# Reading two activations back by blocks, and loading the first expert's gates earlier in the DMA queue

## The chip, the core and the metric

The kernel runs on one core of one Trainium2 chip. The metric is the device time of one execution in microseconds (us), as the median of several runs. The core's engines run side by side and wait for each other by semaphores: PE (TensorE, matrix products; PEld is its loading of weights), DVE (VectorE), ACT (ScalarE), POOL (GpSimd) and SP (SyncE), whose queue issues every DMA of this kernel. A DMA on that queue is issued when all before it have been issued and its own waits are over.

## The reference

Four batches (b = 0 to 3) of 576 tokens go through attention on a memory, a dense layer and four experts:

```python
attn_out = _attn_ref(**attn_kwargs)             # 4 batches x 8 heads x 576 x 64
x = attn_out.transpose(0, 2, 1, 3).reshape(B * S, H * D)   # 2304 x 512
h = x @ w_in                                    # dense: 512 -> 2048
g = np.maximum(h, 0.0) + alpha * np.minimum(h, 0.0)
x = g @ w_out                                   # 2048 -> 512
p = domain_probs / (domain_probs.sum(-1, keepdims=True) + 1e-09)
for e in range(E):                              # four experts, 512 -> 1024 -> 512
    h = np.maximum(x @ w1[e], 0.0)
    out += p[:, e:e + 1] * (h @ w2[e])
```

## The kernel before

**Two stages.** The first stage (attention and the dense layer) is recorded task by task from a string, `ORDER`: each name is a task, and the order of the names is the order of the instructions on every engine. Each float32 operand is split into a high and a low part of a type that PE takes at full rate, and a product is made in three passes (high by high, high by low, low by high); hence the helpers `hi` (ACT) and `lo` (DVE or POOL). The second stage (`run_experts`) is a plain loop. It runs over 32 units: for half 0 (batches 0 and 1) and half 1 (batches 2 and 3), over eight groups of 512 expert columns, over the two batches of the half. Unit 0 is group 0 with batch 0; unit 15 is the last of half 0 (group 7, batch 1), unit 16 the first of half 1 (group 0, batch 2).

**A unit.** It has two passes, hp = 0 and 1. In each, class `Up` makes the first expert product by a seven-product (Strassen-like) scheme on 2 by 2 blocks: `p1` to `p7` write PE's accumulators `ux`, `uy`, `uw`; `v1`, `v16`, `v167` copy or add them into small tiles `v`; `c11`, `c12`, `c21`, `c22` write the four blocks of `h`. `gate` (DVE) multiplies `h` by the tile `p` with the tokens' gates, and `hi` and `lo` split the result into `g`. Between them class `Down` makes the second product of the unit before, eight products `o`, each added to `acc` by `flush`. A product of `Up` is six matmuls (one set) and one of `Down` twelve (two sets), so a unit has 14 + 16 = 30 sets; unit 0, with no unit before it, has 14. Weights go through POOL and ACT in half 0 and are stored to memory (`keep`, tiles `kw`); half 1 reads them back (`w1_load`, `w2_load`).

**Places.** The functions in `more` are recorded at the places (hp, 0) to (hp, 4) of a unit: (hp, 0) follows `v16`, (hp, 1) follows `p2` and `c11`, (hp, 2) follows `v167` and `c22`, (hp, 3) follows the gate of blocks 2 and 3, (hp, 4) follows `p3` and `c12`.

**Activations.** The dense layer's results `y` of batches 2 and 3 don't fit beside the experts' tiles: `spill` stores them (DRAM tiles `ysp2`, `ysp3`), and `unspill` reads each back into one tile `yu` of 128 by 2304 floats (9216 bytes a partition) in a pool `yt` with one buffer. From it class `Combos` makes the seven operands of the scheme: four differences (`sum`, DVE, tiles `xt`) and their splits (`hi` on ACT, `lo` on DVE or POOL, tiles `x`). It does so during unit 15 for batch 2 and unit 16 for batch 3. The tile for batch 3 takes the buffer of batch 2's, so its read waits for the last reader of that.

**Gates.** `store_gates` writes all gates to a DRAM tile `pd` in the first stage. `load_gates(e, b)` reads those of expert e and batch b into a tile `p` of 128 by 576. The first two calls stand at the head of `run_experts`, so their DMAs stand on SP behind all that `ORDER` recorded: behind the load of raw weights `raww21`, the store of the split weights `kw101` (1792 KB, line L713), and `ysp3` (1152 KB).

**Memory.** `to_experts` closes the first stage's pools and opens the experts' pools in the same bytes (`hp`, `vp` and `pp` hold `h`, `v` and `p`). A new tile waits for the last users of the old tiles whose bytes it takes.

Of the kernel before, what the change touches and what calls it, by code (L numbers as in the profile page):

```python
# [8 lines left out]
F32 = mybir.dt.float32  # L9
# [12 lines left out]
HB = S // 2  # L22
# [148 lines left out]
n125 v124 h124 v125 x1h5 d123  # L171
l124 h125 x1l5 x1h6 l125 u126 e123 u127 n126 n127 v126 d124
x1l6 h126 x1h1 v127 d125
l126 h127 x1l1 x1h2 l127 to wh01 d126
x1l2 d127
wl01 e127 sp3
"""
# [14 lines left out]
def memory_attention_experts(ctx: ExitStack, tc: tile.TileContext, phi, q, kv, w_in, w_out, w1, w2, alpha, dp, out):  # L192
# [7 lines left out]
    nc = tc.nc  # L200
# [21 lines left out]
    def unit(name, dt=F32, pool=big):  # L222
        return pool.tile([128, UNIT], dt, tag="big", name=name)
# [289 lines left out]
    wp_t, pw_t, y_t, x_t = {}, {}, {}, {}  # L513
# [106 lines left out]
    B11, T2, T1, B21, T3, T4, B22 = range(7)  # L620
    y_spill = {b: dram.tile([128, UNIT], F32, name=f"ysp{b}") for b in (2, 3)}
# [2 lines left out]
    def spill(b):  # L624
        nc.sync.dma_start(out=y_spill[b], in_=y_t[b].rearrange("p d n -> p (d n)"))

    def unspill(b):
        y_t[b] = unit(f"yu{b}", pool=pools["y"]).rearrange("p (d n) -> p d n", d=4)
        nc.sync.dma_start(out=y_t[b].rearrange("p d n -> p (d n)"), in_=y_spill[b])

    def operand(b, i):

# [5 lines left out]
    class Combos:  # L638
# [3 lines left out]
            self.b, self.t = b, {}  # L642

        def block(self, i, j):
            return y_t[self.b][:, 2 * i:2 * i + 2, j * HB:(j + 1) * HB]

        def sum(self, n):
# [26 lines left out]
    pools = {}  # L674
# [4 lines left out]

    def to_experts():  # L680
        early.close()
        for name, key, bufs in (("w1b", ("w1", 1), 1), ("hp", "h", 2), ("vp", "v", 1), ("pp", "p", 2), ("ring2", "w2", 6), ("accp", "acc", 2), ("yt", "y", 1), ("xt", "xt", 2)):
            pools[key] = ctx.enter_context(tc.tile_pool(name=name, bufs=bufs, reuse_waits="tile"))

    sums_t, kept_t = {}, {}
# [48 lines left out]
    def load_gates(e, b):  # L734
        t = p_t[e, b] = pools["p"].tile([128, S], F32, tag="p", name=f"p{e}{b}")
        src = pd.rearrange("e p i -> e (p i)")[e:e + 1, b * S:(b + 1) * S]
        nc.sync.dma_start(out=t, in_=src.to_broadcast([128, S]))
# [122 lines left out]
                nc.sync.dma_start(out=out[rows, b * S:(b + 1) * S], in_=acc_t[b][:, d])  # L860

    def run_experts():
        load_gates(0, 0)
        load_gates(0, 1)
        units = [(half, g, 2 * half + t) for half in range(2) for g in range(NG) for t in range(2)]
        last, old = None, None
        for n_unit, (half, g, b) in enumerate(units):
            t = b % 2

            more = {}  # L870
            after = units[n_unit + 1:n_unit + 3]
            if t == 0 and n_unit and not half:
                more[0, 1] = [(w1_hi, g, 1)]
                more[0, 2] = [(w1_lo, g, 1)]
            if t == 1 and len(after) > 1:
                nh, ng = units[n_unit + 1][:2]
                if nh:
                    for hp in range(2):
                        more[hp, 1] = [(w1_load, g, ng, hp, 0, 2), (w1_load, g, ng, hp, 3, 5)]
                        more[hp, 3] = [(w1_load, g, ng, hp, 5, 6), (w1_load, g, ng, hp, 2, 3)]  # L880
                        more[hp, 4] = [(w1_load, g, ng, hp, 6, 7)]
                else:
                    more[0, 3] = [(w1_sums, ng, 0)]
                    more[1, 0] = [(w1_hi, ng, 0)]
                    more[1, 1] = [(w1_lo, ng, 0)]
                    more[1, 4] = [(w1_sums, ng, 1)]
            w2 = [(w2_load if half else w2_split, g, hp) for hp in range(2)]
            if t == 0:
                more.setdefault((1, 1), []).extend(f + (0,) for f in w2)
            else:  # L890
                more.setdefault((0, 0), []).extend(f + (1,) for f in w2)
            if n_unit > 1:

                h0, g0, b0 = units[n_unit - 1]
                h1, g1, b1 = units[n_unit + 1] if n_unit + 1 < len(units) else (None, None, None)
                if g0 % 2 == 1 and h1 is not None:
                    more.setdefault((0, 0), []).append((load_gates, g1 // 2, b1))
            if (half, g) == (0, 1) and t == 0:
                more.setdefault((0, 4), []).append((unspill, 2))
            for bb, u0 in ((2, (0, NG - 1, 1)), (3, (1, 0, 0))):  # L900
                if (half, g, t) == u0:
                    x = Combos(bb)
                    parts = [
                        ((0, 0), [(x.sum, 0), (x.sum, 1), (x.hi, B11)]),
                        ((0, 1), [(x.lo, B11, nc.gpsimd), (x.hi, T2), (x.hi, T1)]),
                        ((0, 2), [(x.lo, T1, nc.vector), (x.sum, 2), (x.lo, T2, nc.gpsimd)]),
                        ((0, 3), [(x.sum, 3), (x.hi, B21), (x.hi, T4)]),
                        ((0, 4), [(x.lo, B21, nc.gpsimd), (x.lo, T4, nc.vector)]),
                        ((1, 0), [(x.hi, T3)]),
                        ((1, 1), [(x.lo, T3, nc.vector)]),  # L910
                        ((1, 2), [(x.hi, B22)]),
                        ((1, 3), [(x.lo, B22, nc.vector)] + ([(unspill, 3)] if bb == 2 else [])),
                    ]
                    for place, fs in parts:
                        more.setdefault(place, []).extend(fs)

            for hp in range(2):
                u = Up(g, b, hp)
                side = iter(range(0, 3) if hp == 0 else range(3, 8))

                def down():
                    if old:
                        n = next(side)
                        old.product(n)
                        old.flush(n)

                def extra(place):
                    for f, *args in more.get((hp, place), ()):
                        f(*args)

                u.p1()
                u.p6()
                u.v1()
                if last:

                    if hp == 0:
                        last.hi(1)
                    last.gate(0)
                    last.hi(0)
                u.v16()  # L940
                if last:
                    if hp == 0:
                        last.lo(1, nc.vector)
                    last.lo(0, nc.vector if hp == 0 else nc.gpsimd)
                extra(0)
                if hp == 1:
                    down()
                u.p5()
                u.p2()
                u.c11()  # L950
                if hp == 1:
                    down()
                extra(1)
                u.p7()
                u.v167()
                u.c22()
                extra(2)
                down()
                u.p4()
                u.c21()  # L960
                u.gate(1)
                if hp == 0:
                    u.hi(1)
                    u.lo(1, nc.gpsimd)
                extra(3)
                down()
                u.p3()
                u.c12()
                extra(4)
                down()  # L970
                last = u
            old = Down(g, b)
        last.gate(0)
        for i in (1, 0):
            last.hi(i)
            last.lo(i, nc.vector)
        for n in range(8):
            old.product(n)
            old.flush(n)
# [18 lines left out]
    def task(name, fn, *args):  # L998
        tasks[name] = fn, args
# [66 lines left out]
    for kind in ("in", "out"):  # L1066
        for i in range(DFF // 128):
            d = Decode(kind, i)
            parts = [d.sign, d.first, d.second, d.third, d.add] + ([] if kind == "in" else [d.split, d.split2])
# [6 lines left out]
    task("pst", store_gates)  # L1076
    task("wopen", open_w1)
    task("to", to_experts)

    with tc.manual_schedule():  # L1080
        make_identity(nc, ident)
        nc.gpsimd.memset(mask, 0.0)
        for h in range(4):
            nc.gpsimd.memset(mask[32 * h:32 * h + 32, h % 2:h % 2 + 1], 1.0)
        for name in ORDER.split():
            run(name)
        run_experts()
# [45 lines left out]
```

## Time and profile before

| | before |
|---|---|
| median of 3 runs | 1193.4 us (1193.06 to 1196.33) |
| profiled execution: its own time, its span | 1195.45 us, 1193.6 us |
| mean granted TensorE clock, share of full speed | 0.989 |
| PE busy | 1165.7 us, 98% of the span |
| DVE, ACT, POOL busy | 62%, 35%, 25% |
| DMA | 157.98 MB moved, 37.2% of 16 engines' span |

The span reaches from the first to the last instruction; the time around it is 1.85 us. Busy shares are means over the whole span; what a stage waits for is in the rows below. Lines are those of the kernel before (L841 is a line of `Down.product`).

### The profile page before, as it was taken

Reading aid. Unit: us, or ns where it says so; the run is one execution under the profiler, and the core shown is the slowest. Engines: PE = TensorE matmul, PEld = TensorE weight load, DVE = VectorE, ACT = ScalarE, POOL = GpSimd, SP = SyncE. Lnnn points to the kernel's source line nnn. Section 1 sums busy time; section 2 is a strip of 40 time slices with the busy share of each in tenths; the row PEclk is TensorE's granted clock in tenths of the full one; section 3 lists DMA queues with packets and bytes.
Section 4 is the critical chain, followed back from the end, with each engine's and each line's share of the span. In section 5 each row is a group of like instructions: output and inputs, shape, how many; then the busy total and the mean of one; then the engine's idle time right before and its main releaser. Section 6 shows DMA issues by size and latency. Waiting matters only on the chain.

```text
span 1193.6 us, 21493 instructions
## 1 busy us (share of the span) xinstructions
PE 1165.7 (98%) x8796; PEld 1122.0 (94%) x8796; DVE 744.9 (62%) x1403; ACT 422.9 (35%) x953; POOL 302.3 (25%) x263
## 2 busy tenths in 40 slices
PE   8899999999999899999999999989999999999998
PEld 7578999999999899999999999989999999999998
DVE  6999888885567544656556566665455455545553
ACT  5567665554455334232223232322221111111110
POOL 2332023221010062553434525421001100110010
PEclk9999999999999989999999999989999999999999
DMA  9641121301000446445454444544353433433411
GB/s 378 256 172 27 64 90 53 107 22 77 1 1 4 175 128 230 175 164 197 166 174 172 168 170 163 191 163 165 131 152 123 133 126 93 156 113 138 160 46 70
DMA packets 51667, 157.98 MB, mean 132 GB/s; under 512 B 5360, under 2 KB 18672, under 8 KB 47600
## 3 DMA queue, kind: packets, MB, share of 16 engines
q1 hardware_dynamic: 51568, 156.60, 37.2%
q8 instruction: 69, 1.13, 0.4%
q14 instruction: 30, 0.25, 0.1%
HBM read 103.33 MB, written 53.25 MB: 131 GB/s over the span
## 4 chain that ended last, share of the span: by engine, by line
PE 92%; DVE 4%; DMA 2%; issue 1%; ACT 1%; SPq 0%; POOL 0%; DVEq 0%; ACTq 0%; POOLq 0%
PE o L841 34%; PE y L600 16%; PE uy L750 13%; PE ux L750 8%; PE uw L750 8%; PE h L562 8%; PE pw L523 2%; DMA rawin<-in_w_in 1%; DMA p<-pd 1%; DMA yu<-ysp 1%; DVE xt L660 1%; PE y L597 1%; PE pm L325 0%; PE pc L357 0%; DVE rs L395 0%
## 5 line engine op out<-in xcount | busy, mean ns | idle before, releaser
L853 DVE TENSOR_TENSOR acc<-o,acc 128x288 f32<-128x288 f32 x224 | 102.4, 457 | 202.8 <-PE o L841 202.8
L841 PE MATMUL o<-g,w 128*128 128x288 f32 x1536 | 226.8, 297 | 0.0
L841 PE MATMUL o<-g,w2l 128*128 128x288 f32 x1536 | 223.6, 295 | 1.1 <-DVE g L232 1.1
L841 PEld LDWEIGHTS o<-g,w 128*128 128x128 f32 x1536 | 212.8, 190 | 0.0
L841 PEld LDWEIGHTS o<-g,w2l 128*128 128x128 f32 x1536 | 210.0, 188 | 1.6 <-DVE g L232 1.6
L600 PE MATMUL y<-g,wout 128*128 128x288 f32 x1440 | 205.5, 297 | 0.0
L600 PEld LDWEIGHTS y<-g,wout 128*128 128x128 f32 x1440 | 194.2, 188 | 10.5 <-issue 7.0
L750 PE MATMUL uy<-x,w 128*128 128x288 f32 x1152 | 186.3, 297 | 8.2 <-DVE v L784 8.2
L232 POOL TENSOR_TENSOR g<-h,g 128x576 fp32r<-128x576 f32 x64 | 92.3, 1444 | 388.5 <-ACT g L819 388.5
L750 PEld LDWEIGHTS uy<-x,w 128*128 128x128 f32 x1152 | 165.3, 190 | 9.3 <-DVE v L784 9.3
L788 ACT COPY v<-ux 128x288 f32<-128x288 f32 x64 | 25.6, 401 | 308.3 <-PE ux L750 308.3
L819 ACT CAST g<-h 128x576 fp32r<-128x576 f32 x128 | 83.3, 676 | 138.6 <-DVE h L813 138.6
L750 PE MATMUL ux<-x,w 128*128 128x288 f32 x768 | 124.0, 297 | 4.8 <-ACT v L788 4.8
L750 PE MATMUL uw<-x,w 128*128 128x288 f32 x768 | 123.3, 296 | 0.0
L750 PEld LDWEIGHTS ux<-x,w 128*128 128x128 f32 x768 | 109.9, 190 | 5.0 <-ACT v L788 5.0
L813 DVE SCALAR_TENSOR_TENSOR h<-h,p 128x576 f32<-128x576 f32 x128 | 104.7, 818 | 8.8 <-DMA p<-pd 5.6
L750 PEld LDWEIGHTS uw<-x,w 128*128 128x128 f32 x768 | 109.6, 189 | 0.0
L232 POOL TENSOR_TENSOR w<-raww,w 128x512 fp32r<-128x512 f32 (+1 forms) x48 | 74.5, 1566 | 137.8 <-ACT w L507 77.6
L562 PE MATMUL h<-a,wp 128*128 128x288 f32 x720 | 108.8, 296 | 0.1
L784 DVE TENSOR_TENSOR v<-uy,v 128x288 f32<-128x288 f32 x128 | 58.6, 457 | 80.5 <-PE uy L750 80.2
L562 PEld LDWEIGHTS h<-a,wp 128*128 128x128 f32 x720 | 99.5, 188 | 2.7 <-issue 1.3
L581 DVE SCALAR_TENSOR_TENSOR pos<-neg,nal,pos 128x288 f32<-128x288 f32 x120 | 64.8, 544 | 43.0 <-ACT pos L576 42.4
(117 smaller groups left out, 1125.4 us busy)
## 6 DMA issues: line engine op xcount, KB each, us to landing
kw<-w SPq DMA_DIRECT2D x16, 1792.0 KB, 7.2
raww<-in_w SPq DMA_DIRECT2D x32, 512.0 KB, 4.0
kw<-w SPq DMA_DIRECT2D x32, 512.0 KB, 2.9
w<-kw SPq DMA_DIRECT2D x32, 512.0 KB, 4.8
w2l<-kw SPq DMA_DIRECT2D x32, 512.0 KB, 4.5
w<-kw SPq DMA_DIRECT2D x48, 256.0 KB, 3.8
kv<-in_kv SPq DMA_DIRECT2D x8, 1152.0 KB, 12.0
rawin<-in_w_in SPq DMA_DIRECT2D x16, 512.0 KB, 3.7
```

The costliest lines, as they stand in the source:

```text
L232: eng.tensor_tensor(out=out, in0=in0, in1=in1.bitcast(F32), op=ALU.subtract)
L523: mm(p[64 * j:64 * j + 64, g * 256:(g + 1) * 256], vt_t[b, g][:, j, :], win_t[c][:, 2 * g + j, e * 256:(e + 1) * 256], start=True, stop=True,)
L562: mm(p, wp_t[b, c, f // 2][:, x, o2 + g * 256:o2 + g * 256 + 128], a_t[b][:, y, g, o:o + HB], start=(n == 0), stop=(n == 5))
L581: nc.vector.scalar_tensor_tensor(out=pos, in0=neg, scalar=nal[:, ft:ft + 1], in1=pos, op0=ALU.mult, op1=ALU.add)
L600: mm(First.acc[d], w[:, x, d * 128:(d + 1) * 128], self.gt[:, y, 0:HB], start=(self.start and n == 0), stop=(self.stop and n == 2))
L750: mm(p, w[:, x, a, k], operand(self.b, i)[:, y, k], start=(start and n == 0), stop=(n == 5), skip_group_check=not start)
L784: nc.vector.tensor_tensor(out=out, in0=x, in1=y, op=ALU.add)
L788: nc.scalar.copy(out=self.v1_t, in_=self.x)
L813: nc.vector.scalar_tensor_tensor(out=h, in0=h, scalar=0.0, in1=p_t[self.g // 2, self.b], op0=ALU.max, op1=ALU.mult)
L819: nc.scalar.copy(out=g_t[self.g, self.b, self.hp][:, i, 0], in_=h)
L841: mm(self.p, w[:, x, i, d % 2 * 128:(d % 2 + 1) * 128], g, start=(m == 0), stop=(m == 11))
L853: nc.vector.tensor_tensor(out=a, in0=self.p, in1=a, op=ALU.add)
```

## The change

`pp` is opened ahead of `hp` and `vp`, so the tiles `p` take other bytes of the closed pools. The two loads of the first expert's gates become tasks `pg0` and `pg1` in `ORDER`, right behind `to`, and leave the head of `run_experts`. `yt` gets four buffers of a quarter each, and `unspill` reads one quarter (a block of 128 by 2 by 288, 288 KB, in runs of 1152 bytes). Batch 2's four blocks are read at one place as before (unit 2). Batch 3's are read at four places of unit 15, (0, 2), (0, 4), (1, 1) and (1, 4), in place of one read at (1, 3).

```diff
-l126 h127 x1l1 x1h2 l127 to wh01 d126
+l126 h127 x1l1 x1h2 l127 to pg0 pg1 wh01 d126
...
-    def unspill(b):
-        y_t[b] = unit(f"yu{b}", pool=pools["y"]).rearrange("p (d n) -> p d n", d=4)
-        nc.sync.dma_start(out=y_t[b].rearrange("p d n -> p (d n)"), in_=y_spill[b])
+    def unspill(b, i, j):
+        t = y_t[b, i, j] = pools["y"].tile([128, 2, HB], F32, tag="y", name=f"yu{b}{i}{j}")
+        src = y_spill[b].rearrange("p (d n) -> p d n", d=4)
+        nc.sync.dma_start(out=t, in_=src[:, 2 * i:2 * i + 2, j * HB:(j + 1) * HB])
...
         def block(self, i, j):
+            if self.b > 1:
+                return y_t[self.b, i, j]
             return y_t[self.b][:, 2 * i:2 * i + 2, j * HB:(j + 1) * HB]
...
-        for name, key, bufs in (("w1b", ("w1", 1), 1), ("hp", "h", 2), ("vp", "v", 1), ("pp", "p", 2), ("ring2", "w2", 6), ("accp", "acc", 2), ("yt", "y", 1), ("xt", "xt", 2)):
+        for name, key, bufs in (("w1b", ("w1", 1), 1), ("pp", "p", 2), ("hp", "h", 2), ("vp", "v", 1), ("ring2", "w2", 6), ("accp", "acc", 2), ("yt", "y", 4), ("xt", "xt", 2)):
...
     def run_experts():
-        load_gates(0, 0)
-        load_gates(0, 1)
...
-                more.setdefault((0, 4), []).append((unspill, 2))
+                more.setdefault((0, 4), []).extend((unspill, 2, i, j) for i in range(2) for j in range(2))
...
-                        ((1, 3), [(x.lo, B22, nc.vector)] + ([(unspill, 3)] if bb == 2 else [])),
+                        ((1, 3), [(x.lo, B22, nc.vector)]),
                     ]
+                    if bb == 2:
+                        parts += [(place, [(unspill, 3, i, j)]) for place, i, j in (((0, 2), 0, 0), ((0, 4), 0, 1), ((1, 1), 1, 0), ((1, 4), 1, 1))]
...
+    for b in range(2):
+        task(f"pg{b}", load_gates, 0, b)
```

The orders of PE, DVE, ACT and POOL stay as they were. Only SP's order changes. At the border of the stages it was as follows (`p00` and `p01` are the gates of expert 0 for batches 0 and 1, `kw2000` is the first store of unit 0's split weights):

```order
L713 DMA kw100_3455<-w100_3433 128x3584
L625 DMA ysp2_108<-y2_1498 128x2304
L438 DMA raww21_5110<-in_w2 128x1024
L713 DMA kw101_5112<-w101_5080 128x3584
L625 DMA ysp3_109<-y3_1787 128x2304
L737 DMA p00_5119<-pd_107 128x576
L737 DMA p01_5121<-pd_107 128x576
L713 DMA kw2000_5222<-w2000_5219 128x1024
```

After the change the two gate loads stand ahead of `raww21`, `kw101` and `ysp3`, right behind `ysp2`:

```order
L717 DMA kw100_3455<-w100_3433 128x3584
L625 DMA ysp2_108<-y2_1498 128x2304
L741 DMA p00_5080<-pd_107 128x576
L741 DMA p01_5082<-pd_107 128x576
L438 DMA raww21_5114<-in_w2 128x1024
L717 DMA kw101_5116<-w101_5084 128x3584
L625 DMA ysp3_109<-y3_1787 128x2304
L717 DMA kw2000_5222<-w2000_5219 128x1024
```

In unit 15, SP reads group 0's weights back (`w170`, `w171`) and stores parts of the output (`out_0`). Before, the one read of batch 3's activation stood near the end of these:

```order
L720 DMA w170_8585<-kw100_3455 128x2x256 x2
L860 DMA out_0<-acc0_5328 128x576
L720 DMA w170_8585<-kw100_3455 128x2x256
L860 DMA out_0<-acc0_5328 128x576
L720 DMA w171_8747<-kw101_5112 128x2x512 x2
L860 DMA out_0<-acc0_5328 128x576
L720 DMA w171_8747<-kw101_5112 128x2x256 x2
L629 DMA yu3_9218<-ysp3_109 128x2304
L720 DMA w171_8747<-kw101_5112 128x2x256
L860 DMA out_0<-acc0_5328 128x576
L737 DMA p03_9281<-pd_107 128x576
```

Now three of four blocks stand further ahead, and the last one stands behind the last piece of `w171`:

```order
L631 DMA yu300_9047<-ysp3_109 128x2x288
L724 DMA w170_8591<-kw100_3455 128x2x256 x2
L864 DMA out_0<-acc0_5328 128x576
L724 DMA w170_8591<-kw100_3455 128x2x256
L631 DMA yu301_9106<-ysp3_109 128x2x288
L864 DMA out_0<-acc0_5328 128x576
L724 DMA w171_8753<-kw101_5116 128x2x512 x2
L631 DMA yu310_9191<-ysp3_109 128x2x288
L864 DMA out_0<-acc0_5328 128x576
L724 DMA w171_8753<-kw101_5116 128x2x256 x3
L631 DMA yu311_9252<-ysp3_109 128x2x288
L864 DMA out_0<-acc0_5328 128x576
```

## Rows read from the trace of the kernel before

**Rows 1.** Waits, longest in total first: engine, line, waited for, us, times, longest.

```profile
PE uy L750 <- DVE v L784: 8.2, 4, 5.2
...
DVE h L813 <- DMA p<-pd: 5.6, 1, 5.6
```

**Rows 2.** One unit each (0, 1, 13, 15, 16): length, engines' busy us, PEclk, DMA.

```profile
404.89:425.45 20.56, 14.67 (x86) 13.86 (x85) 7.97 (x17) 3.88 (x8) 5.57 (x4) 0.79 0.63 239
425.45:449.94 24.49, 24.49 (x181) 24.49 (x181) 11.95 (x20) 9.32 (x19) 14.68 (x13) 0.97 0.52 166
712.11:735.94 23.83, 23.83 (x183) 23.83 (x181) 13.98 (x25) 6.73 (x12) 14.25 (x13) 1.00 0.45 166
...
759.77:787.27 27.50, 25.64 (x182) 25.41 (x181) 21.54 (x32) 9.16 (x17) 11.40 (x7) 0.94 0.62 208
787.27:818.45 31.18, 25.94 (x182) 25.70 (x181) 20.40 (x32) 8.22 (x15) 7.57 (x5) 0.89 0.38 126
```

**Rows 3.** Timeline, border of the stages: start, us, engine, instruction [idle before <-releaser].

```profile
374.06 1.76 PE L562 MATMUL h<-a,wp 128*128 128x288 f32 x12
...
387.03 0.33 SPq L625 DMA_DIRECT2D ysp<-y  x1
...
396.94 1.76 PE L562 MATMUL h<-a,wp 128*128 128x288 f32 x12
...
409.58 1.06 PE L750 MATMUL uy<-x,w 128*128 128x288 f32 x6 [0.55 <-DVE v L784]
...
410.68 0.46 DVE L784 TENSOR_TENSOR h<-uy,v 128x288 f32<-128x288 f32 x1 [0.67 <-PE uy L750]
...
418.61 1.81 PE L750 MATMUL ux<-x,w 128*128 128x288 f32 x6 [4.79 <-ACT v L788]
```

**Rows 4.** Chain that ended last, in order of time: start, us, what.

```profile
407.08 9.55 DMA p<-pd
...
785.48 9.55 DMA yu<-ysp
```

**Rows 5.** Timeline of unit 16, from its first gates' split to PE's restart.

```profile
788.60 1.25 ACT L819 CAST g<-h 128x576 fp32r<-128x576 f32 x2
...
789.50 1.42 DVE L232 TENSOR_TENSOR g<-h,g 128x576 fp32r<-128x576 f32 x2
...
791.24 1.76 PE L841 MATMUL o<-g,w 128*128 128x288 f32 x12
...
795.06 0.76 DVE L660 TENSOR_TENSOR xt<-yu 128x576 f32<-128x576 f32 x1 [4.14 <-DMA yu<-ysp]
...
795.80 1.40 POOL L232 TENSOR_TENSOR x<-yu,x 128x576 fp32r<-128x576 f32 x1 [16.27 <-ACT x L668]
795.85 1.97 DVE L660 TENSOR_TENSOR xt<-yu,xt 128x576 f32<-128x576 f32 x1
797.74 0.45 DVE L784 TENSOR_TENSOR v<-uy,v 128x288 f32<-128x288 f32 x1
...
798.24 1.81 PE L750 MATMUL uy<-x,w 128*128 128x288 f32 x6 [5.24 <-DVE v L784]
...
801.34 0.45 DVE L853 TENSOR_TENSOR acc<-o,acc 128x288 f32<-128x288 f32 x1
```

**Rows 6.** Stretches around idle times of PE, in Rows 2's columns.

```profile
765.50:767.36 1.86, 0.01 (x1) 0.01 (x1) 1.80 (x2) 0.39 (x1) 1.86 (x2) 1.00 0.77 308
768.25:771.75 3.50, 3.50 (x17) 3.50 (x16) 3.44 (x4) 0.00 (x0) 1.33 (x1) 0.52 0.66 171
...
64.76:66.01 1.25, 0.00 (x1) 0.00 (x0) 1.25 (x4) 1.02 (x2) 0.00 (x0) 1.00 0.00 0
```

**Rows 7.** DMA issues, 782 to 796 us: KB each, median us to landing.

```profile
w<-kw SPq DMA_DIRECT2D x3, 256.0 KB, 3.2
out<-acc SPq DMA_DIRECT2D x2, 288.0 KB, 5.3
p<-pd SPq DMA_DIRECT2D x1, 288.0 KB, 8.4
```

## The prediction

> **What bounds the kernel now.** I read the wait list first, then a window for each unit, then the timeline at the two places that stand out. In the experts' stage PE is the bound: unit 13 takes 23.83 us and PE is busy in all of it [rows 2]. Its 30 sets of six matmuls make 23.83 / 30 = 0.794 us a set. What can be won there is only what a unit takes beyond its sets. Four units do. Unit 0 has 14 sets, 11.12 us, and takes 20.56: 9.44 over. Unit 1 is 0.66 over. Unit 15 takes 27.50, 3.67 over, and unit 16 takes 31.18, 7.35 over [rows 2]. Together that is 21.1 us. The wait list names what stands behind two of them: a gate on DVE that waits 5.6 us for the DMA of `p`, and PE's `uy` that waits for an add on DVE, 5.2 us at the longest [rows 1].
>
> At the border the chain runs through that DMA: it is issued at 407.08 and lands 9.55 us later, at 416.63 [rows 4], and only then the gate runs. It could have run when the add before it was done, at 410.68 + 0.46 = 411.14 [rows 3]. Behind the gate, in program order, stand on DVE `c12`, the second gate and `v16`, and on ACT the split of the gated blocks and then `v1`, the copy for which PE's next `ux` waits: PE stands still for 4.79 us [rows 3]. The clock falls too, and unit 0's mean granted clock is 0.79 [rows 2].
>
> In unit 16 the read of batch 3's activation is issued at 785.48 and takes 9.55 us [rows 4]. The two differences on DVE start at 795.06, the add `v167` behind them ends at 798.19, and PE's `uy` has waited for it for 5.24 us [rows 5].
>
> **The gates.** The two loads move ahead of `raww21`, `kw101` and `ysp3`, to directly behind `ysp2`, which SP issues at 387.03 [rows 3]. In their new bytes the last old tiles are the end of a dense weight and a folded weight of the last step but ten, whose products stand at 374.06 in the trace [rows 3], so nothing holds them there. Even at the landing time that they had among 3 MB of other transfers, 9.55 us [rows 4], they are there before 400, more than 10 us ahead of the gate at 411.14. What stands behind them on SP (`raww21`, `kw101`, `ysp3`) waits for work on POOL and DVE that is not done by then, so two issues of 0.33 us [the row at 387.03, rows 3] cost nothing; uncovered, that would be 0.7 us. The tiles `h` and `v` take other bytes too; the last products to read the old tiles there start at 396.94 and are over by 398.70 [rows 3], and the first write of `h` or `v` comes after 404.89, when the experts begin. Cover 6 us, cost nothing.
>
> What is late next in unit 0? Not `v1`: with the gate at 411.14 to 411.91, the split on ACT (1.25 us for two, so 0.63 each [rows 5]) ends at about 412.6 and `v1` (0.4 us) at 413.0, while PE has sets until 418.61 - 4.79 = 413.82 [rows 3]. What stays is the wait that each pass of unit 0 has for `v167`, because no second product lies between `p7` and `p4`. In the first pass five sets start before the one at 409.58: 409.58 - 404.89 - 5 x 0.794 = 0.72 us [rows 2, 3]. Two of them make 1.44. So unit 0 gains 9.44 - 1.44 = **8.0 us**, and unit 1 its 0.66, which is the low clock's tail. Bounds: at least PE's idle 4.79, at most all 10.1.
>
> **The blocks.** Batch 2's four reads in unit 2 land some 300 us before unit 15 needs them; SP pays three more issues there. In unit 15 each block of batch 3 is read as soon as its buffer's last reader is done. The first three are issued before 785 and land under unit 15. Only the last matters: block (1,1), whose last reader is the DVE `lo` that also released the one read at 785.48. It stands behind one more piece of `w171`, so I put its issue at 786.4. How long 288 KB in runs of 1152 bytes takes, the trace doesn't show. The nearest rows in this stretch are 3.2 us for 256 KB of weights, 5.3 for 288 KB of output and 8.4 for 288 KB of gates [rows 7]. I take 5.3, since the block has that size: it lands at 791.7, bounds 789.6 and 794.8.
>
> With the data there, DVE is free for the first difference at 789.50 + 1.42 = 790.92, and ACT for the split of block (0,0) at 788.60 + 1.25 = 789.85 [rows 5]. That split lets POOL's `lo` of the same block start. Now a row against a free ride: a difference alone took 0.76 us, but 1.97 when POOL's `lo` (1.40 us, from 795.80) ran beside it; it ended 0.62 us after POOL did [rows 5]. I expect the same here: POOL from 790.92 to 792.32, the first difference to 792.94, the second to 793.70, `v167` ends 0.37 later (as 798.19 stands to 797.82), and `uy` starts at 794.1. PE's product before it ends at 791.24 + 1.76 = 793.0 [rows 5]. So 1.1 us of wait stay out of 5.24. Without the collision the differences end at 792.44 and PE doesn't wait.
>
> The Trainium skill ("SBUF — State Buffer", "Who interferes with whom") says that a DVE instruction with two SBUF inputs and a GpSimd instruction that reads SBUF hold one shared port in turn, each for its whole length. By that rule 1.1 us stays whichever of the two starts first; without it the sum below would be 1.1 us better. The row of 1.97 agrees with it.
>
> The next wait: the third `o` of the unit needs the bank of the first, which is free when `flush` ends at 801.34 + 0.45 = 801.79, 3.6 us after `v167` [rows 5]. PE has four sets (3.18 us) from `uy` to there. At 794.05 + 3.6 = 797.65 against 794.1 + 3.18 = 797.28 that is 0.4 us; 0.45 with the start. Before, the low clock hid it.
>
> The clock: after 1.86 us of idle in unit 15 it was granted at 0.52 for 3.5 us, but after 1.25 us at 64.76 it stayed at 1.00 [rows 6]. 1.1 is nearer to the second, so I take no fall; a fall would cost about 3.67 - 1.86 = 1.8 us [rows 2, 6]. Unit 16 is then 1.55 over and gains 7.35 - 1.55 = **5.8 us**. Bounds: 3.67, if it looks like unit 15, and 7.35.
>
> **The sum.** 8.0 + 0.66 + 5.8 = 14.5 us. The profiled execution took 1195.45 (span 1193.6 and 1.85 around it), which gives 1181.0. It lies 2.05 above the median, within the three runs; from the median of 1193.4 it is **1178.9 us**.
>
> **Rivals.**
> 1. *The clock falls in unit 16, or the last block is late.* For the first speaks the fall after 1.86 us of idle, against it 1.25 without one [rows 6]. For the second speak the 8.4 us of `p` [rows 7] and that the four blocks put 0.9 MB more into the time before 785. At 794.8 the second difference ends at 795.56 and `uy` starts at 796.0: 3.0 of idle and 1.8 of clock, 4.8 over and a gain of 2.5. The two give 1180.7 to 1182.2.
> 2. *Splitting the read gains nothing.* Four reads in short runs, each behind others in one queue, could take longer than one of 1152 KB; then only the gates pay: 1193.4 - 8.7 = 1184.7. Against it: three of four are issued before the old read's time, and the last has a quarter of the bytes. The Trainium skill ("DMA: Bandwidth & Descriptors", "Bandwidth") advises DMAs of at least 1 MiB, which speaks against the split; by its fit of 2.0 us + bytes / 436e3 per us, made for another issuing engine, I estimate 2.7 us for a block and 10.7 for four in a row, against 4.7 for the whole. The trace's 9.55 for the whole differs from that figure.
> 3. *The gates' part doesn't come*, because something else holds ACT or DVE at 412: 1193.4 - 5.8 = 1187.6. Nothing in the timeline stands there.
> 4. *Slower.* SP stands at block (1,0) until POOL has read its old block, and the last pieces of `w171`, the outputs and the next gates are queued behind it. PE needs `w171` in unit 16's second pass, 13 sets (10.3 us) and the 1.55 of waits after 787.27, at 799.1; issued at 785.9 and 5.3 us on its way [rows 7], it is there at 791.2. If that wait lasted 8 us longer, PE would begin to wait, and each further us would cost one; from 8 + 14.5 = 22 us on the kernel is slower. At 30 us it would be 1193.4 + 7.5 = 1201. Nothing in unit 15 holds POOL so long: it is busy in 11.40 of 27.50 us [rows 2].
>
> **How the numbers follow.** Forecast 0.64, rival 1 0.18, rival 2 0.07, rival 3 0.04, a change that does nothing to be measured 0.03, rival 4 0.04. The bounds of the terms give 1193.4 - 17.5 = 1175.9 (all that is over in units 0, 1 and 16) and 1193.4 - 4.8 - 3.7 = 1184.9 (idle alone in unit 0, unit 16 like unit 15). The range 1175.9 to 1185 takes in rivals 1 and 2 and leaves 0.11 out. Less than 0.3% (3.6 us) can't be told from no change here; the forecast and rivals 1 to 3 are beyond it: faster 0.93, same 0.03, slower 0.04.
>
> **What would show it.** Right: the gate no longer waits for `p`, unit 0 takes about 12.6 us at a clock of 1.00, unit 16 about 25.4, with one wait of `uy` near 1 us and a difference stretched to about 2 us beside POOL; unit 15 still takes 27.5. Wrong: a gate that waits still, a wait for `yu` in unit 16, a granted clock of 0.5 after its idle time, or PE waiting for `w` in units 16 and 17.

## The result and the profile after

| | before | after |
|---|---|---|
| median | 1193.23 us (4 runs, 1190.82 to 1196.33) | 1181.62 us (4 runs, 1181.30 to 1181.89) |
| profiled execution: own time, span | 1195.45, 1193.6 | 1181.37, 1179.6 |
| mean granted clock | 0.989 | 0.997 |

The ratio is 0.9901, with an interval of 0.9878 to 0.9924: faster by 0.8 to 1.2%. The time lies in the range, 2.7 us above the 1178.9 forecast.

The wait list after (columns as in [rows 1]) no longer has a gate that waits for `p`, and PE's longest wait for the add `v` fell from 5.2 to 1.9 us, which is the one in unit 15. A short wait for `flush` (L857) is new:

```profile
PE uy L754 <- DVE v L788: 4.0, 4, 1.9
...
PE o L845 <- DVE acc L857: 0.8, 2, 0.7
```

Units 0, 1, 13, 15 and 16 after, in the columns of [rows 2]:

```profile
405.32:418.09 12.77, 11.67 (x86) 11.20 (x85) 7.40 (x17) 3.88 (x8) 4.90 (x4) 1.00 0.71 278
418.09:441.92 23.83, 23.83 (x182) 23.83 (x181) 12.94 (x20) 9.41 (x19) 15.22 (x14) 1.00 0.60 204
703.93:727.76 23.83, 23.83 (x182) 23.83 (x181) 13.98 (x25) 6.72 (x12) 14.24 (x13) 1.00 0.44 162
...
751.76:778.63 26.87, 24.36 (x183) 23.89 (x181) 21.56 (x32) 8.94 (x17) 11.45 (x7) 1.00 0.69 238
778.63:804.24 25.61, 24.37 (x182) 23.90 (x181) 20.29 (x32) 8.01 (x15) 7.92 (x5) 1.00 0.39 127
```

Against [rows 2] these are -7.79, -0.66, 0, -0.63 and -5.57 us, together -14.65. The first stage gives 0.43 back (unit 0 starts at 405.32, not 404.89). That leaves -14.2, and the two profiled executions differ by 1195.45 - 1181.37 = 14.1.

The border after, as in [rows 3]. The gates are issued behind `ysp2`, 19 us earlier than the load in [rows 4]; the gate at 411.59 waits for nothing, and only the two short waits of `uy` are left:

```profile
387.42 0.33 SPq L625 DMA_DIRECT2D ysp<-y  x1
387.85 1.34 SPq L741 DMA_DIRECT2D p<-pd  x2
...
410.00 1.06 PE L754 MATMUL uy<-x,w 128*128 128x288 f32 x6 [0.55 <-DVE v L788]
...
411.59 0.76 DVE L817 SCALAR_TENSOR_TENSOR h<-h,p 128x576 f32<-128x576 f32 x1
...
416.39 1.07 PE L754 MATMUL uy<-x,w 128*128 128x288 f32 x6 [0.55 <-DVE v L788]
```

Unit 16 after, as in [rows 5]. The last block (`yu311`) is issued at 777.85. POOL's split of block (0,0) starts at 781.86 and ends at 783.57. DVE's first difference beside it takes 2.00 us and ends at 784.19, 0.62 behind POOL. The second takes 0.76, the add follows, and `uy` has waited 1.05 us:

```profile
777.85 0.55 SPq L631 DMA_DIRECT2D yu<-ysp  x1
...
781.11 0.68 ACT L672 CAST x<-yu 128x576 fp32r<-128x576 f32 x1
...
781.86 1.71 POOL L232 TENSOR_TENSOR x<-yu,x 128x576 fp32r<-128x576 f32 x1 [10.30 <-ACT x L672]
...
782.19 2.00 DVE L664 TENSOR_TENSOR xt<-yu,yu 128x576 f32<-128x576 f32 x1
...
784.23 0.76 DVE L664 TENSOR_TENSOR xt<-yu,xt 128x576 f32<-128x576 f32 x1
784.90 0.45 DVE L788 TENSOR_TENSOR v<-uy,v 128x288 f32<-128x288 f32 x1
...
785.40 1.06 PE L754 MATMUL uy<-x,w 128*128 128x288 f32 x6 [1.05 <-DVE v L788]
...
789.03 1.87 PE L845 MATMUL o<-g,w 128*128 128x288 f32 x12 [0.19 <-DVE acc L857]
```

### The profile page after: what moved, and what is told of

Read it like the earlier page. It is cut to its first block, busy times and chain, and to the rows that moved or that the text cites. A ratio compares the mean times of both kernels' runs of the same rounds, so it can differ in the third digit from the quotient of the medians.

```text
span 1179.6 us, 21508 instructions
## 1 busy us (share of the span) xinstructions
PE 1158.2 (98%) x8796; PEld 1114.4 (94%) x8796; DVE 745.0 (63%) x1403; ACT 422.2 (36%) x953; POOL 302.5 (26%) x263
## 4 chain that ended last, share of the span: by engine, by line
PE 93%; DVE 4%; DMA 1%; ACT 1%; issue 0%; SPq 0%; POOL 0%; DVEq 0%; ACTq 0%; POOLq 0%
PE o L845 34%; PE y L600 17%; PE uy L754 13%; PE ux L754 8%; PE uw L754 8%; PE h L562 8%; PE pw L523 3%; DMA q<-in_q 1%; DVE xt L664 1%; PE pc L357 1%; PE y L597 0%; PE pm L325 0%; DMA w<-kw 0%; PE warm L246 0%; DVE x L232 0%
## 5 line engine op out<-in xcount | busy, mean ns | idle before, releaser
L857 DVE TENSOR_TENSOR acc<-o,acc 128x288 f32<-128x288 f32 x224 | 102.2, 456 | 201.0 <-PE o L845 201.0
L845 PEld LDWEIGHTS o<-g,w 128*128 128x128 f32 x1536 | 210.3, 188 | 1.3 <-DVE acc L857 1.3
## 6 DMA issues: line engine op xcount, KB each, us to landing
kv<-in_kv SPq DMA_DIRECT2D x8, 1152.0 KB, 12.6
```

The costliest lines, as they stand in the source:

```text
L845: mm(self.p, w[:, x, i, d % 2 * 128:(d % 2 + 1) * 128], g, start=(m == 0), stop=(m == 11))
L857: nc.vector.tensor_tensor(out=a, in0=self.p, in1=a, op=ALU.add)
```

## The experiments

The theory to be tested is that of the prediction: the gates and the blocks act at two places apart, so their gains add; of the blocks' part the earlier issue counts; and what stays in unit 16 is the collision of DVE with POOL. The rivals: one part alone brings the whole, the split into four is worth most by itself, or the 1.05 us that stay are a late last block. All these kernels compute the whole reference.

| kernel | median, us | ratio to before, interval | unit 0 | unit 15 | unit 16 |
|---|---|---|---|---|---|
| gates_only | 1185.91 | 0.9930, 0.9917 to 0.9942 | 12.76 | 27.49 | 30.44 |
| blocks_only | 1189.20 | 0.9962, 0.9949 to 0.9976 | 19.05 | 27.50 | 25.61 |
| gates_oldbytes | 1185.14 | 0.9922, 0.9908 to 0.9935 | 12.77 | 26.87 | 28.95 |
| before_look2 | one execution, 1194.21 | | 19.22 | 27.50 | 30.45 |
| after_again | 1181.40 | 0.9894, 0.9872 to 0.9915 | 12.76 | 27.50 | 25.60 |
| blocks_late | 1183.88 | 0.9917, 0.9898 to 0.9935 | 12.77 | 27.49 | 27.75 |
| split_later | 1181.80 | 0.9900, 0.9884 to 0.9917 | 12.76 | 26.87 | 25.89 |
| early_sums | 1178.60 | 0.9871, 0.9853 to 0.9889 | 12.77 | 24.22 | 25.70 |
| early_sums_again | 1178.42 | 0.9877, 0.9855 to 0.9899 | 12.76 | 24.24 | 25.48 |
| late_lo | 1176.96 | 0.9858, 0.9837 to 0.9878 | 12.77 | 24.20 | 24.38 |

The units are from start to start in the profiled execution of each. The first four kernels ran on one chip (median of before 1193.86), the next four on another (1194.99), the last two on a third (1194.83).

### The two parts apart (gates_only, blocks_only)

gates_only keeps the whole reads of batches 2 and 3. Its line for batch 3, against the kernel after:

```diff
-                        ((1, 3), [(x.lo, B22, nc.vector)]),
+                        ((1, 3), [(x.lo, B22, nc.vector)] + ([(unspill, 3)] if bb == 2 else [])),
```

> Only the gates' part: the two loads stand behind ysp2 and pp is opened first; batch 2 and 3 are read back whole, as before. Theory (the parts add, each is worth what its own units show): unit 0 takes 12.8 us instead of 20.56, unit 16 still 31, and 8.4 us less than before by the profiled executions. Rival (the change lost 2.7 us of the forecast 14.5 somewhere in the gates' part, for example by what SP issues later): unit 0 or 1 longer than 12.8 and 23.8. By medians I expect 1186 to 1187 if before's profiled execution was a slow one by 2 us, 1184.7 if it was not.

blocks_only puts the gate loads back to the head of `run_experts`, and the pools back into the old order:

```diff
-l126 h127 x1l1 x1h2 l127 to pg0 pg1 wh01 d126
+l126 h127 x1l1 x1h2 l127 to wh01 d126
```

> Only the blocks: the gates are loaded at the head of the experts and the pools stand in the old order. Theory: unit 0 takes 20.6 us as before, unit 16 25.6, 5.6 us less than before by the profiled executions, and the two parts' gains add up to that of the whole change within 1 us. Rival (splitting the read gains nothing): unit 16 stays near 31 and the time within 1 us of before.

In the timeline of gates_only the read is late as before, though it landed after 8.0 us here, not 9.55, and so the wait is 3.68, not 5.24:

```profile
776.62 0.33 SPq L629 DMA_DIRECT2D yu<-ysp  x1
...
784.63 0.76 DVE L660 TENSOR_TENSOR xt<-yu 128x576 f32<-128x576 f32 x1 [2.57 <-DMA yu<-ysp]
...
787.81 0.61 PE L750 MATMUL uy<-x,w 128*128 128x288 f32 x1 [3.68 <-DVE v L784]
```

In the wait list of blocks_only the gate and PE wait at the border:

```profile
PE ux L754 <- ACT v L792: 4.6, 1, 4.6
...
DVE h L817 <- DMA p<-pd: 5.5, 1, 5.5
```

Each part alters its own units and no other. By the profiled executions the two gain 1195.45 - 1185.83 = 9.6 and 1195.45 - 1187.57 = 7.9 us, where 8.4 and 5.6 were expected; but the profiled execution of before lies above its median, and that of blocks_only is the shortest of its five, so the medians decide. By the medians they are worth 1193.86 - 1185.91 = 7.95 and 1193.86 - 1189.20 = 4.66 us, 12.6 together; the whole change measured 11.6 and, in after_again, 13.6. Within the intervals the parts add, and neither brings the whole.

### Do the other bytes matter? (gates_oldbytes)

As gates_only, but `pp` is opened behind `vp`, where it was; the tasks `pg0` and `pg1` stay at their new place.

> The gates' loads move, but pp stays behind vp, so that p takes the bytes of the folded weights that the last steps read. Theory (only the place in SP's order matters): SP stands at the first gate load until PE's last h of the dense layer, some 399 us, which is before raww21 may go at 404; the gates land by 404, unit 0 takes 12.8 us and the time is that of gates_only. Rival (the opening of pp ahead matters): the loads wait longer, raww21 is late, the gate waits again and unit 0 takes 15 us or more.

In those bytes the loads wait for PE's last product `h` with the old tile, which starts at 392.14; SP issues them at 393.98. That is 6 us later than in the kernel after the change and still 17 us ahead of the gate:

```profile
387.00 0.33 SPq L625 DMA_DIRECT2D ysp<-y  x1
...
392.14 1.76 PE L562 MATMUL h<-a,wp 128*128 128x288 f32 x12
...
393.98 0.80 SPq L737 DMA_DIRECT2D p<-pd  x2
...
404.14 0.33 SPq L438 DMA_DIRECT2D raww<-in_w  x1
```

Unit 0 takes the same 12.77 us and the median is 0.8 below that of gates_only, with intervals that overlap; what the profiled execution gains on that of gates_only lies in units 15 and 16 (2.1 us), not in unit 0. The order of the pools is worth nothing that can be measured; the place in SP's order is the whole of this part.

### How much does one profile say? (before_look2, after_again)

The kernel before, unchanged, profiled once more; and the changed kernel, unchanged, timed and profiled again.

> The kernel before, a second profiled execution. Theory (its runs differ by what the clock does after the idle times of PE): the stretches in which PE waits are as long as in the first profile (4.8, 1.9 and 5.2 us), but the time at half clock behind them differs, by up to 3 us of span. Rival (the runs differ elsewhere): units 0, 15 and 16 take 20.6, 27.5 and 31.2 again, and the span differs outside them or not at all.

> The changed kernel again, beside the next three on the same chip. Theory (before's runs scatter by what the clock does behind its two long waits of PE, which are gone): its runs lie within 1.5 us of each other, near 1181.6, with units 0, 1 and 16 at 12.8, 23.8 and 25.6; unit 15 takes 26.9 or 27.5, by whether the clock falls behind its wait of 1.86. Rival (the scatter comes from elsewhere): a scatter of 3 us or more, as before.

Units 0 and 1 of before_look2:

```profile
406.43:425.65 19.22, 13.30 (x86) 12.50 (x85) 7.35 (x17) 3.88 (x8) 5.56 (x4) 0.91 0.60 227
425.65:449.48 23.83, 23.83 (x182) 23.83 (x181) 12.43 (x20) 9.33 (x19) 14.64 (x13) 1.00 0.58 193
```

PE stood still for 4.82 us at the border, as in [rows 3], but the mean granted clock of unit 0 is 0.91, not 0.79 [rows 2], and unit 1 has lost nothing. The two units take 43.05 us in place of 20.56 + 24.49 = 45.05. Unit 16 takes 30.45, not 31.18, with a wait of 3.68, not 5.24; the read landed after 8.0 us. These two make 2.7 us; the first stage took 1.5 more (unit 0 starts at 406.43). The execution took 1194.21 in place of 1195.45. So the theory holds at the border: the same idle time, another time at half clock. In unit 16 the wait itself was shorter, which it did not foresee, and the first stage differs too: so far the rival, by which the runs differ elsewhere, has a part.

The 29 runs of the kernel before that were timed beside these experiments, on three chips, fit the clock's part: the nine with a mean granted clock of 0.993 or more took 1190.08 to 1193.91 us, the 20 with 0.991 or less took 1193.44 to 1196.72.

In after_again the units are those of after, but for unit 15: 27.50 at a mean clock of 0.94, as before. Its four runs lie 2.5 us apart (1180.95 to 1183.48), more than the 1.5 of the theory and less than the 3 of the rival. The profiled one is the longest: it starts unit 0 1.56 us later than after does (406.88, not 405.32) and loses 0.63 in unit 15. So the two waits that are gone are not the only source of the scatter.

### Split or early issue? (blocks_late)

All four blocks of batch 3 are read at the last place:

```diff
-for place, i, j in (((0, 2), 0, 0), ((0, 4), 0, 1), ((1, 1), 1, 0), ((1, 4), 1, 1))]
+for place, i, j in (((1, 4), 0, 0), ((1, 4), 0, 1), ((1, 4), 1, 0), ((1, 4), 1, 1))]
```

> Batch 3's activation in four blocks, but all four read at the last place of unit 15, where the last one stands in the changed kernel. Theory (the early issue of three blocks is what pays, not the split): the last block lands about as late as the whole tile did, 7.6 to 9.6 us after the first issue, PE's wait in unit 16 is 3 to 5 us, the unit takes 29 to 31 and the time is about 1185 to 1186. Rival (small pieces land sooner by themselves): a wait of 1 to 2 us and a unit of 25.6 to 27.

```profile
778.14 2.09 SPq L631 DMA_DIRECT2D yu<-ysp  x4
...
783.88 1.73 DVE L664 TENSOR_TENSOR xt<-yu,yu 128x576 f32<-128x576 f32 x1 [1.31 <-DMA yu<-ysp]
785.64 0.76 DVE L664 TENSOR_TENSOR xt<-yu,xt 128x576 f32<-128x576 f32 x1
...
786.82 1.81 PE L754 MATMUL uy<-x,w 128*128 128x288 f32 x6 [2.17 <-DVE v L788]
```

Between theory and rival, and nearer to the rival. The four blocks stand one place behind the old place of the whole read: they are issued 0.78 us ahead of unit 16's start, where the whole read is issued 1.79 ahead in before and in gates_only. Even so they leave a wait of `uy` of 2.17 us, where the whole read left 3.33 to 5.24; unit 16 takes 27.75 where that left 28.95 to 31.18. Issued early they leave 1.05 and 25.61. So splitting alone brings a part, and the early issue 2.1 us more. Of these 2.1 us the wait is 1.1; the rest goes with the clock, which fell behind the wait of 2.17 (0.53 in the 3.5 us from 786.82) and held behind that of 1.05. The blocks landed after 5.2 us each (median of the four), though 288 KB is a quarter of what took 7.6 to 9.55. The Trainium skill ("DMA: Bandwidth & Descriptors", "Bandwidth") advises DMAs of 1 MiB and more, for bandwidth. Here the landing counted, and the smaller reads gave the shorter wait: the first difference needs two blocks, not four.

### The collision taken away (split_later, early_sums, late_lo)

split_later records batch 3's split of block (0,0) (`hi` on ACT, `lo` on POOL) one place later, behind the splits of the two differences:

```diff
-((0, 0), [(x.sum, 0), (x.sum, 1), (x.hi, B11)]),
-((0, 1), [(x.lo, B11, nc.gpsimd), (x.hi, T2), (x.hi, T1)]),
-((0, 2), [(x.lo, T1, nc.vector), (x.sum, 2), (x.lo, T2, nc.gpsimd)]),
+((0, 0), [(x.sum, 0), (x.sum, 1)] + ([(x.hi, B11)] if bb == 2 else [])),
+((0, 1), ([(x.lo, B11, nc.gpsimd)] if bb == 2 else []) + [(x.hi, T2), (x.hi, T1)] + ([(x.hi, B11)] if bb == 3 else [])),
+((0, 2), [(x.lo, T1, nc.vector), (x.sum, 2), (x.lo, T2, nc.gpsimd)] + ([(x.lo, B11, nc.gpsimd)] if bb == 3 else [])),
```

> The changed kernel, with batch 3's split of block (0,0) (high part on ACT, low part on POOL) recorded behind those of the differences, so that POOL does not run beside the two differences. Theory (1.05 us of wait in unit 16 is the collision of POOL's low part with the first difference on DVE): both differences take 0.76 us, PE's uy does not wait or waits under 0.2 us, and unit 16 takes 24.3 to 24.7 instead of 25.6; the time is 1.0 us less than the changed kernel's. Rival (the wait is for the last block's landing): the wait stays at 1 us.

early_sums is split_later with the first two differences of batch 2 moved from unit 15 to the end of unit 14:

```diff
+            if (half, g, t) == (0, NG - 1, 0):
+                x_of[2] = Combos(2)
+                more.setdefault((1, 4), []).extend([(x_of[2].sum, 0), (x_of[2].sum, 1)])
...
-((0, 0), [(x.sum, 0), (x.sum, 1)] + ([(x.hi, B11)] if bb == 2 else [])),
+((0, 0), [(x.hi, B11)] if bb == 2 else [(x.sum, 0), (x.sum, 1)]),
```

> As split_later, and batch 2's first two differences are made at the end of unit 14 instead of in unit 15, where POOL splits weights beside them. Theory (the same collision is the 1.86 us of wait in unit 15): each difference takes 0.76 us in unit 14 and PE does not wait for them, unit 14 stays at 23.8, unit 15 takes 24 to 24.8 instead of 26.9 or 27.5, and the time is 3.5 to 4.5 us less than the changed kernel's, near 1177.5. Rival (other work of DVE and POOL in unit 15 sets the wait): unit 15 gains less than 1 us.

late_lo is early_sums with batch 3's `lo` of block (0,0) moved once more; early_sums ran again beside it:

```diff
-((0, 2), [(x.lo, T1, nc.vector), (x.sum, 2), (x.lo, T2, nc.gpsimd)] + ([(x.lo, B11, nc.gpsimd)] if bb == 3 else [])),
-((0, 3), [(x.sum, 3), (x.hi, B21), (x.hi, T4)]),
+((0, 2), [(x.lo, T1, nc.vector), (x.sum, 2), (x.lo, T2, nc.gpsimd)]),
+((0, 3), ([(x.lo, B11, nc.gpsimd)] if bb == 3 else []) + [(x.sum, 3), (x.hi, B21), (x.hi, T4)]),
```

> As in early_sums, but batch 3's block (0,0) is split on POOL only at (0,3), behind batch 3's third difference in DVE's order. Theory (the third difference was stretched from 0.76 to 1.86 us by the split beside it, and that delayed flush): the difference takes 0.76, flush comes about 1.1 us earlier, the wait of o falls from 1.29 to about 0.2, unit 16 takes 24.6 in place of 25.7, and the median is 1.1 us below early_sums (1177.5). Rival (POOL's split of T2 alone is enough to stretch it, or the late split now stretches the gate or a flush): the wait of o stays above 0.8 or a wait of uy above 0.8 comes in its place, and the time is that of early_sums within 0.4 us.

> early_sums unchanged, beside late_lo on one chip. 1178 to 1179 us, unit 16 25.7 with a wait of o of 1.3 us.

Unit 16 of split_later. Both differences take 0.76 us now. The second waits 0.47 for the last block, and `uy` only 0.24. But POOL's `lo` now lies beside the third difference, which takes 1.86; `flush` behind it is late, and `o` waits 1.29:

```profile
782.67 0.75 DVE L664 TENSOR_TENSOR xt<-yu,yu 128x576 f32<-128x576 f32 x1
...
783.89 0.76 DVE L664 TENSOR_TENSOR xt<-yu,xt 128x576 f32<-128x576 f32 x1 [0.47 <-DMA yu<-ysp]
...
785.07 1.06 PE L754 MATMUL uy<-x,w 128*128 128x288 f32 x6 [0.24 <-DVE v L788]
...
786.82 1.95 POOL L232 TENSOR_TENSOR x<-yu,x 128x576 fp32r<-128x576 f32 x1
787.51 1.86 DVE L664 TENSOR_TENSOR xt<-yu,xt 128x576 f32<-128x576 f32 x1
789.30 0.45 DVE L857 TENSOR_TENSOR acc<-o,acc 128x288 f32<-128x288 f32 x1
...
789.80 1.86 PE L845 MATMUL o<-g,w 128*128 128x288 f32 x12 [1.29 <-DVE acc L857]
```

The wait had moved, and the time stayed where 1.0 us less was expected.

In unit 15 of the kernel after, the two differences of batch 2 stand beside POOL's split of weights and take 1.85 and 1.71:

```profile
754.94 3.37 POOL L232 TENSOR_TENSOR w<-raww,w 128x512 fp32r<-128x512 f32 x2 [8.18 <-ACT w L507]
...
755.33 1.85 DVE L664 TENSOR_TENSOR xt<-yu,yu 128x576 f32<-128x576 f32 x1
...
757.21 1.71 DVE L664 TENSOR_TENSOR xt<-yu,xt 128x576 f32<-128x576 f32 x1
```

At the end of unit 14, in early_sums, POOL stands still beside them:

```profile
750.47 0.75 DVE L664 TENSOR_TENSOR xt<-yu,yu 128x576 f32<-128x576 f32 x1
751.25 0.76 DVE L664 TENSOR_TENSOR xt<-yu,xt 128x576 f32<-128x576 f32 x1
```

With them there, PE waits no more in unit 15, and the median is 2.8 us below that of after_again on the same chip; 3.5 to 4.5 were expected, and unit 16's 1.29 is what is missing. This move took the two differences out of unit 15 as a whole, their own 1.51 us with the 2.05 of stretch; that the stretch alone made the wait of 1.86 is not shown. late_lo takes most of that away: the third difference takes 0.76, and `o` waits 0.18:

```profile
783.03 0.76 DVE L664 TENSOR_TENSOR xt<-yu,xt 128x576 f32<-128x576 f32 x1
783.71 0.45 DVE L857 TENSOR_TENSOR acc<-o,acc 128x288 f32<-128x288 f32 x1
...
784.21 1.87 PE L845 MATMUL o<-g,w 128*128 128x288 f32 x12 [0.18 <-DVE acc L857]
```

Its median is 1176.96, 1.46 below early_sums on the same chip (1.1 were expected, and 1.10 is what unit 16 gained) and below both kernels of the case. Where the collision went, a wait of PE went with it: in split_later and late_lo, where only batch 3's split of block (0,0) moved, and in early_sums with the reserve above; the last block is late only by the 0.47 that DVE shows, and that costs PE 0.24 at most. The Trainium skill ("SBUF — State Buffer", "Who interferes with whom") has a rule on a port that the two engines share, which the prediction weighed. Every one of these rows agrees with it: 0.75 or 0.76 alone, 1.71 to 2.00 beside POOL. That it is the port, no run here shows by itself.

## Why the prediction was right, and which step was off

**The gates: right.** Forecast 12.56 us for unit 0 with two waits of 0.72 left, measured 12.77. The two listed waits are 0.55 each; counted in sets of 0.794 us, as the forecast was, the two products `uy` come 0.71 and 0.83 late. Nothing else held ACT or DVE (rival 3). One part of the change that the prediction went through, the pool order, does not matter.

**The blocks: right.** Forecast 25.38 us for unit 16, measured 25.61. The last block was put 0.87 us ahead of the unit's start and was issued 0.78 ahead; it landed in 5.7 us, where 5.3 was taken. The waits forecast were 1.1 for `uy` and 0.45 for `o`; the profile lists 1.05 and 0.19. The 0.45 was counted in sets, and counted so it came true: 789.03 - 785.40 - 4 x 0.794 = 0.45. That the clock would not fall after this wait held in after, after_again and blocks_only (1.05 each). The ground for it was thin: the row at 64.76 [rows 6] shows the clock during the idle time only. (It stayed at 1.00 in the 3.5 us behind it too, from 66.01 on.)

**Unit 15: half right.** 27.5 was forecast. It is 26.87 in after and 27.50 in after_again, after the same wait of 1.86 us. Where the clock holds, `o` waits 0.65 for `flush` in its place, so the difference is only 0.63.

**The sum: the step that was off** is the last one, "It lies 2.05 above the median, within the three runs; from the median of 1193.4 it is 1178.9 us". Against the profiled execution the sum gave 1181.0, and the profiled execution after took 1181.37, the medians 1181.62 and 1181.40. Going on to the median took off another 2.05 us, and these did not come. Two things on record bear on it.

The first: what was long in that execution of before lay in the very places that the change mends. The 14.5 us hold a half-clock tail at the border that was 2.0 us longer than in before_look2 (45.05 against 43.05 in units 0 and 1), and a read of `yu` that landed 1.55 later than there (unit 16: 31.18 against 30.45). With before_look2's units the same steps would have given 19.22 - 12.56 = 6.66 for unit 0, nothing for unit 1, and 30.45 - 25.38 = 5.07 for unit 16: 11.7 us. So part of the 2.05 stood in the 14.5 already. How often the long tail comes is not settled: of three profiles in which this wait stands (before, before_look2, blocks_only), one has it. That the median of gates_only lies 8.0 us below before, where units 0 and 1 of before_look2 hold 43.05 - 36.6 = 6.45 to win, suggests that it is no rarity.

The second: the median of 1193.4 came from three runs. Beside the experiments the medians of before are 1193.86 (9 runs), 1194.99 (11) and 1194.83 (9), so the profiled execution lies 0.5 to 1.6 above these, not 2.05. The gain by medians is 11.6 us in the result and 13.6 beside after_again. The 11.7 of before_look2, taken from 1193.4, would have given 1181.7; that this meets the measured 1181.62 is in part luck. How the missing 2.7 us divide between the long execution and the low median stays open.

Of the rivals, 1 (1180.7 to 1182.2) holds the measured number by its size, but not by its mechanism: neither did the clock fall nor was the last block late. Rival 2 falls with blocks_only and blocks_late; rival 4 shows nowhere: PE waits for no `w` in units 16 and 17.

## What to carry to other kernels

A load that everything behind a border waits for belongs at the place in the queue where its buffer comes free, not where its user stands in the code; here two names in the order were worth 8 us, by the medians of gates_only. When an operation on a shared resource is moved out of the way of the one on the path, look which operation it meets next: only the second move paid. When a profiled execution lies off the median, look whether it is off in the places that the change mends, and work out the gain from a second profile, before any of it is taken from the median. And take that median from more than three runs.

## What the runs showed of the hardware

The same idle time of PE was followed by different clocks. After 1.86 us in unit 15 the clock fell in six of nine profiled executions (27.5 us for the unit) and held in three (26.87). A stretch of after_again and then the same one of after, from 0.89 us behind the start of `uy`:

```profile
761.78:765.28 3.50, 3.50 (x17) 3.50 (x16) 3.44 (x4) 0.00 (x0) 1.34 (x1) 0.53 0.69 176
```

```profile
760.23:763.73 3.50, 2.85 (x22) 2.62 (x21) 3.46 (x4) 0.00 (x0) 1.36 (x1) 1.00 0.51 156
```

The idle time itself reads alike in before [rows 6] and in after, where the clock held (1.86 us, PE without work, DMA share 0.77):

```profile
757.48:759.34 1.86, 0.01 (x1) 0.00 (x0) 1.81 (x2) 0.39 (x1) 1.86 (x2) 1.00 0.77 308
```

At the border, behind 4.65 to 4.82 us of idle time, the half clock lasted for two products of PE in before_look2 (from 420.17) and in blocks_only (3.60 us, granted 0.53), but until 426.8 in before, some 8 us from PE's restart at 418.61. There the granted clock was 0.50 from about 416.7 on, 2 us ahead of the restart. No row that was read here tells ahead which way it goes.
